# Attention and MLP decode step: each 8 MiB block as two half-transfers from two issuing engines

## The chip, the cores and the metric

The kernel runs on one core of one Trainium2 chip. Its time is device microseconds of one execution, the median of three runs. A separate execution was recorded by the hardware profiler; every number below that speaks of a line, an engine or a wait comes from that one.

## What is computed

One decode step for two sequences. A layer norm of `x` feeds two branches whose results are added to `x`: grouped-query attention over a cache of 32768 positions (32 query heads, 4 key/value heads, head size 128), and an MLP with SiLU.

```
xn  = layernorm(x)                                   # x: (2, 1, 1024)
q   = (xn @ wq) as 32 heads of 128
p   = softmax(q . k_cache * 128**-0.5)               # k_cache, v_cache: (2, 4, 32768, 128)
att = (p . v_cache) as 4096 @ wo
mlp = silu(xn @ w1) @ w2                             # w1: (1024, 3584), w2: (3584, 1024)
out = x + att + mlp
```

All of it is float32. The two caches are 268 MB, the weights some 63 MB; every byte is read once.

## The kernel before, in words

**Blocks and buffers.** The host lays out all weights and the cache as blocks of 128 rows of up to 16384 float32 (64 KiB a row, 8 MiB a block). On the chip there are two buffers of that shape, `buf[0]` (bufA) and `buf[1]` (bufB), one row per partition. Blocks alternate between them, in this order: two blocks of `wq`; `w1b` (three quarters of a block) and `w1a`; for each of the eight pairs of key/value head and sequence, two blocks of keys and two of values; two blocks of `wo`; `w2a`, in two transfers; `w2b`, in seven transfers of falling size. That makes 40 steps (`STEPS`), 20 turns of bufA and bufB.

**Loads.** SyncE issues them all (lines 110, 118 and the function `load`, L169 to L172). Each transfer of a block adds 16 to the semaphore of its buffer, `ld[0]` or `ld[1]`, when it is complete. Before it issues block n, SyncE waits until block n-2, which was in the same buffer, has been used up: `step(n)` (L166) names the semaphore and its value, `turn_sem` for the first two and `freed` for the others, which VectorE raises (`relay`, L218, through `pass_on`, L44) when TensorE has said that it is done. Two loads stand out. `x` itself (32 KiB, to every 16th partition of `xs`) is issued by ScalarE (L116), after GpSimd has cleared `xs`; and the second block is issued by SyncE only when `x` has landed (the semaphore `ldx`, L117).

**TensorE** loops over the turns. `taken(k)` (L314) waits until `ld[k]` holds 16 and takes them off again, then does the same with `tok[k]`, which says that the stationary operand `wt[k]` is ready. `slots(k, ...)` (L300) then multiplies: 64 matmuls of 128 x 32 by 128 x 512 for a full block, into the two halves of the PSUM tile `xy`. Small matmuls for the softmax follow each pair of key blocks and each pair of value blocks.

**ScalarE** works through a list in order: the issue of `x`; one square root for the layer norm (L141); for the first four blocks a copy of the PSUM result to `ev[n]` (L190 to L197); the sigmoid's exponential (L230); a copy of the queries (L239); then, for each of the eight attention rounds, a wait for `subbed` and two exponentials that make the weights for the value blocks (L245), and a wait for `normed` and a copy of the round's result, `onew` (L248); and at the end the copies of the last results (L254, L256). **VectorE** does the softmax's reductions (`attend`), **GpSimd** sets up the stationary operands (`stage`).

**The end.** The parts of `w2a` and `w2b` after the first have semaphores of their own, `more` and `last`. SyncE writes the result (L389) when ScalarE has copied it (L256).

Of the kernel before, what the change touches and what calls it, by code (L numbers as in the profile page):

```python
# [11 lines left out]
W = 16384  # L12
# [6 lines left out]
STEPS = 4 + 4 * LOOPS + 4  # L19
PAIRS = STEPS // 2  # L20
# [31 lines left out]
def gqa_plus_mlp_kernel(nc, x8, kt, v0, v1, wq, wo, w1a, w1b, w2a, w2b, out):  # L52


    pe, dve, act, pool = (Stream(nc, e, n) for e, n in
                          ((nc.tensor, "pe"), (nc.vector, "dve"), (nc.scalar, "act"), (nc.gpsimd, "pool")))
    sp, T, V, A, G = nc.sync, nc.tensor, nc.vector, nc.scalar, nc.gpsimd
    sems = [pe.sem, dve.sem, act.sem, pool.sem]

    def sem(name):  # L60
        sems.append(nc.alloc_semaphore(name))
        return sems[-1]

    def sb(name, *shape):
        return nc.alloc_sbuf_tensor(name, shape, F32).ap()
# [4 lines left out]
    buf = [sb(n, P, W) for n in ("bufA", "bufB")]  # L70
    ld, more, tok = ([sem(f"{n}{k}") for k in "AB"] for n in ("ld", "more", "tok"))
    ldx, turn_sem = (sem(n) for n in ("ldx", "marks"))
    freed, subbed, normed, tq, pself = (sem(n) for n in ("freed", "subbed", "normed", "tq", "pself"))
    trm, tgd, tls, tob = (sem(n) for n in ("trm", "tgd", "tls", "tob"))
# [39 lines left out]
    z = pool.mark(G.memset(blank, 0.0))  # L114
    act.wait(z_x)
    A.dma_start(xs[::16, :], x8).then_inc(ldx, 16)  # L116
    sp.wait_ge(ldx, 16)  # L117
    sp.dma_start(buf[1], wq[1]).then_inc(ld[1], 16)

    pool.wait(z)  # L120
    t = pool.mark(G.affine_select(out=ident, in_=ident, compare_op=ALU.not_equal, fill=1.0, base=0,
# [44 lines left out]
    def step(n):  # L166
        return (turn_sem, n) if n <= 2 else (freed, n - 2)

    def load(k, dst, src, s, n):  # L169
        if n:  # L170
            sp.wait_ge(*step(n))
        sp.dma_start(buf[k][:, dst] if isinstance(dst, slice) else dst, src).then_inc(s, 16)  # L172

    every = slice(0, W)
    load(0, slice(0, 3 * W // 4), w1b, ld[0], 1)
    load(1, every, w1a, ld[1], 2)
    for it in range(LOOPS):
        h, b = divmod(it, B)
        for j, src in enumerate((kt[b, h, 0], kt[b, h, 1], v0[b, h], v1[b, h])):
            load(j % 2, every, src, ld[j % 2], 3 + 4 * it + j)  # L180
    load(0, every, wo[0], ld[0], STEPS - 5)
    load(1, every, wo[1], ld[1], STEPS - 4)
    load(0, slice(0, W // 2), w2a[:, :W // 2], ld[0], STEPS - 3)
    load(0, slice(W // 2, W), w2a[:, W // 2:], more[0], 0)
    cuts = [0, 6 * D, 8 * D, 9 * D, 10 * D, 11 * D, 11 * D + 4 * CUT, 12 * D]
# [3 lines left out]

    for n in range(4):  # L190
        act.wait(step(n + 1))
        if n == 2:
            A.copy(ev[n][:, :512], ps[0][:, :512])
            A.copy(ev[n][:64, 512:], ps[0][:64, 512:])
            t = act.mark(A.copy(ev[n][64:96, 512:], ps[0][96:, :512]))
        else:
            t = act.mark(A.copy(ev[n], ps[n % 2]))  # L197
        if n == 1:
            pool.pass_on(tok[n], 1, t)
        else:  # L200
            pool.wait(t)
        a, b = ev[n][:, :512], ev[n][:, 512:]
        if n == 0:
            G.tensor_add(sumq[:, :512], a, b).then_inc(tok[n], 1)
        elif n == 1:
            i_sumq = pool.mark(G.tensor_add(sumq[:, 512:], a, b))  # L206
        elif n == 2:
            t = pool.mark(G.tensor_add(sumh[:96, 512:], a[:96, :384], b[:96, :384]))
            for j in range(3):
                pool.wait(t)  # L210
                t = pool.mark(G.tensor_add(sumh[96:, 512 + P * j:512 + P * (j + 1)], a[32 * j:32 * j + 32, 384:],
                                           b[32 * j:32 * j + 32, 384:]))
            shifted = t
        else:
            pool.wait(shifted)
            i_sumh = pool.mark(G.tensor_add(sumh[:, :512], a, b))
# [23 lines left out]
           tqs[:, :, ::16].rearrange("p (h m) b -> p h b m", m=REP)).then_inc(tq, 1)  # L240
    for it in range(LOOPS):
        h, b = divmod(it, B)
        act.wait((subbed, it + 1))
        for c in range(NC):
            A.activation(wt[c].rearrange("p e m -> p (e m)"), st[:, 1024 * c:1024 * c + 1024], AF.Exp,  # L245
                         scale=SCALE).then_inc(tok[c], 1)
        act.wait((normed, it + 1))
        A.copy(oT[:, REP * h:REP * (h + 1), 16 * b], onew).then_inc(tq, 1)  # L248
    for s in (trm, tgd):
# [1 line left out]
    outs = []  # L251
    for n in range(3):
        act.wait(step(STEPS - 3 + n) if n < 2 else (turn_sem, 5))
        outs.append(act.mark(A.copy(ev[n], ps[n % 2])))  # L254
    act.wait((pe, 2))
    i_ot = act.mark(A.copy(ot, acc))  # L256
# [55 lines left out]
        return m  # L312

    def taken(k):  # L314
        pe.take(ld[k], 16)
        pe.take(tok[k])

    engine = [T.engine]
# [1 line left out]
    T.reg_mov(pair, 0)  # L320
    T.reg_mov(half, 0)
    pe.wait(i_const)
    for s, n in ((trm, 1), (tgd, 1), (tls, 1), (tob, 1), (more[0], 16 * PAIRS - 16), (more[1], 16 * PAIRS - 16)):
        T.sem_inc(s, n)
    T.br("te_loop")

# [4 lines left out]
    with nc.body("te_loop", valid_engines=engine):  # L331
        again = T.mark_branch_hint_location()
        taken(0)
        slots(0, (0, 1)).then_inc(turn_sem, 1)
        taken(1)
        slots(1, (0,))
        T.br_eq(pair, PAIRS - 1, on_true="te_rest", on_false="te_more")
# [131 lines left out]
```

## Time and profile before

| | us |
|---|---|
| median of three runs | 772.4 (772.36 to 772.52) |
| the profiled execution | 772.44 |
| its span, first to last recorded work | 771.1 |
| TensorE matmuls, busy | 392.9 |
| TensorE weight loads, busy (beside the matmuls) | 125.9 |
| VectorE, busy | 133.3 |
| GpSimd, busy | 44.2 |
| ScalarE, busy | 29.0 |

The transfers moved 331.40 MB in 6816 packets, 430 GB/s over the span.

How to read the profile: PE is TensorE's matmuls, PEld its weight loads, DVE is VectorE, ACT is ScalarE, POOL is GpSimd, SP is SyncE; a name with a q (SPq, ACTq) is that engine's queue of instructions that are not counted as busy, such as the issue of a transfer. `bufA<-in_kt` means that bufA is written from the input `kt`. q1 is the queue of the transfers that SyncE issued, q10 that of those that ScalarE issued. In a row of the timeline stand the start and the duration in microseconds, then engine, line and operation, and in brackets how long the engine had been idle and what ended that. In a row of waits stand the total, the number of times and the longest. In the page's slices the span is cut into 40 equal parts.

### The profile page before, as it was taken

To read this page: it belongs to the slowest core of one execution; us is meant where nothing else is said; L and a number is where in the kernel's file an instruction comes from. 1 tells how busy PE (TensorE), PEld (TensorE's weight loads), DVE (VectorE), ACT (ScalarE), POOL (GpSimd) and SP (SyncE) were. 2 spreads that over 40 slices of the span, in tenths; PEclk is the share of its full clock that TensorE was granted. 3 is DMA by queue.
4 is the path that set the end of the run, shared out by engine and by line. 5 is a ranking of instruction groups with operands and counts; after the bars stand their busy time and mean duration, and the time that the engine had idled before them with its cause. 6 is when DMAs were issued, how large, how long until landed. Compare 5 with 4: busy or idle time off the path is not lost. (4 is left out here: it accounts for less than half of the span.)

```text
span 771.1 us, 6114 instructions
## 1 busy us (share of the span) xinstructions
PE 392.9 (51%) x2702; PEld 125.9 (16%) x2702; DVE 133.3 (17%) x100; ACT 29.0 (4%) x39; POOL 44.2 (6%) x65
## 2 busy tenths in 40 slices
PE   0454554464545454645464545454645455545476
PEld 0111111121112111211121112111211121112122
DVE  2000104030403030304030303031303030313000
ACT  0000100100010001000100010001000100010000
POOL 3001200001000000010001000100010001000121
PEclk9977667767677767677767677767677767677689
DMA  9999999999999999999999999999999999999997
GB/s 382 435 435 435 435 435 435 435 435 435 435 435 435 435 435 435 435 435 435 435 435 435 435 432 435 425 428 418 425 432 435 432 435 435 435 435 435 435 433 329
DMA packets 6816, 331.40 MB, mean 430 GB/s; under 512 B 776, under 2 KB 920, under 8 KB 1440
## 3 DMA queue, kind: packets, MB, share of 16 engines
q1 hardware_dynamic: 6800, 331.37, 99.5%
q10 hardware_dynamic: 16, 0.03, 0.0%
HBM read 331.38 MB, written 0.02 MB: 430 GB/s over the span
## 5 line engine op out<-in xcount | busy, mean ns | idle before, releaser
L107 PE MATMUL xy<-bufB,weights 128*32 128x512 f32 x1248 | 181.8, 747 | 166.6 <-PEq L49 166.6
L107 PE MATMUL xy<-bufA,weights 128*32 128x512 f32 x1280 | 178.2, 718 | 100.4 <-PEq L49 100.4
L107 PEld LDWEIGHTS xy<-bufB,weights 128*32 128x32 f32 x1248 | 49.7, 134 | 298.8 <-issue 298.7
L107 PEld LDWEIGHTS xy<-bufA,weights 128*32 128x32 f32 x1280 | 49.9, 129 | 212.1 <-issue 212.1
L268 DVE STREAM_TRANSPOSE st<-xy 128x2048 f32<-128x2048 f32 x8 | 18.5, 2317 | 241.5 <-PE xy L107 241.5
L278 DVE TENSOR_REDUCE blank<-xy 128x512 f32<-128x2048 f32 x8 | 18.3, 2292 | 224.5 <-PE xy L107 224.5
L290 POOL MEMSET weights<- 128x2048 f32 x8 | 14.4, 1805 | 526.9 <-POOLq L49 526.9
L107 PE MATMUL smA<-blank 128*8 128x128 f32 x20 | 5.4, 370 | 51.9 <-PEq L49 51.9
L107 PE MATMUL smA<-blank,ones 128*128 128x8 f32 x18 | 4.9, 347 | 50.6 <-PEq L49 50.6
L269 DVE TENSOR_REDUCE blank<-st 128x8 f32<-128x2048 f32 x8 | 30.5, 3808 | 0.3
L279 DVE TENSOR_REDUCE blank<-weights 128x8 f32<-128x2048 f32 x8 | 30.4, 3798 | 0.0
L245 ACT ACTIVATE weights<-st 128x1024 f32<-128x1024 f32 x16 | 16.0, 1048 | 326.6 <-DVE st L275 326.6
L275 DVE TENSOR_TENSOR st<-st,gmax 128x2048 f32<-128x2048 f32 x8 | 18.3, 2292 | 0.3
L107 PE MATMUL smB<-blank 128*128 128x8 f32 x72 | 15.9, 349 | 0.0
L107 PEld LDWEIGHTS smB<-blank 128*128 128x128 f32 x72 | 15.6, 317 | 0.0
L107 PEld LDWEIGHTS smA<-blank,ones 128*128 128x128 f32 x18 | 4.3, 298 | 58.5 <-issue 58.5
L248 ACT COPY blank<-onew 128x8 f32<-128x8 f32 x8 | 1.6, 204 | 279.4 <-DVE onew L282 279.4
L107 PEld LDWEIGHTS smA<-blank 128*8 128x8 f32 x20 | 1.3, 89 | 60.2 <-issue 60.2
L384 DVE TENSOR_TENSOR rest<-ev 128x512 f32<-128x512 f32 x1 | 0.7, 693 | 49.1 <-POOL ev L382 49.1
L296 POOL COPY weights<-qall 128x128 f32 x32 | 8.0, 295 | 3.1 <-POOL weights L290 3.1
L107 PE MATMUL smB<-blank,ones 8*128 8x8 f32 x20 | 5.3, 333 | 5.7 <-PEq L49 5.7
L222 DVE STREAM_TRANSPOSE tqs<-sumq 128x1024 f32<-128x1024 f32 x1 | 1.2, 1245 | 38.2 <-POOL sumq L206 38.2
(59 smaller groups left out, 59.4 us busy)
## 6 DMA issues: line engine op xcount, KB each, us to landing
bufA<-in_w2a SPq DMA_DIRECT2D x2, 4096.0 KB, 24.0
bufA<-in_w1b SPq DMA_DIRECT2D x1, 6144.0 KB, 24.8
bufB<-in_w2b SPq DMA_DIRECT2D x1, 3072.0 KB, 16.5
bufB<-in_w2b SPq DMA_DIRECT2D x3, 512.0 KB, 20.2
bufB<-in_w2b SPq DMA_DIRECT2D x1, 1024.0 KB, 18.6
bufB<-in_w2b SPq DMA_DIRECT2D x1, 384.0 KB, 21.5
bufA<-in_kt SPq DMA_DIRECT2D x8, 27.7
bufB<-in_kt SPq DMA_DIRECT2D x8, 28.9
```

What stands on the lines that cost most here:

```text
L107: return T.matmul(o, lhsT, rhs, start=start, stop=stop)
L222: i_q = dve.mark(V.transpose(tqs.rearrange("p c m -> p (c m)"), sumq))
L245: A.activation(wt[c].rearrange("p e m -> p (e m)"), st[:, 1024 * c:1024 * c + 1024], AF.Exp, scale=SCALE).then_inc(tok[c], 1)
L248: A.copy(oT[:, REP * h:REP * (h + 1), 16 * b], onew).then_inc(tq, 1)
L268: then(3, V.transpose(st, xy))
L269: V.tensor_reduce(rm, e8.rearrange("p n m -> p m n"), AX.X, ALU.max).then_inc(trm, 1)
L275: V.tensor_sub(e8, e8, gmax.to_broadcast([P, 256, REP])).then_inc(subbed, 1)
L278: V.tensor_reduce(ob, xy.rearrange("p (c n) -> p n c", c=4), AX.X, ALU.add).then_inc(tob, 1)
L279: V.tensor_reduce(lsum, weights.rearrange("p e (r m) -> p m (e r)", m=REP), AX.X, ALU.add).then_inc(tls, 1)
L290: G.memset(weights, 0.0).then_inc(pself, 1)
L296: m = G.tensor_copy(o, q[:, None, None, :].to_broadcast([P, 4, 4, REP]))
L384: t = dve.mark(V.tensor_add(rest, ev[0][:, :512], ev[0][:, 512:]))
```

## The change

Every block from the second up to the last of `wo` (numbers 1 to 37, counted from 0) is now brought by two transfers of 64 rows each into the same buffer. SyncE issues the even partitions, ScalarE the odd ones. Both add 16 to the buffer's semaphore, so TensorE now takes 32 off it. The first block, `w2a` and `w2b` remain single transfers of SyncE's; for those that `taken` waits for, the missing 16 are added by hand: by TensorE at the start for the first block, by ScalarE at the end for `w2a` and for the first part of `w2b`.

ScalarE's issues are written into its list by hand, each behind its own wait on `step`: the odd rows of the second block right after `x` (behind a wait for `ldx`, as on SyncE); those of the next four blocks ahead of the four copies to `ev[n]`; in each attention round two ahead of the wait for `subbed` and two between the exponentials and the wait for `normed`.

```diff
-    sp.wait_ge(ldx, 16)
-    sp.dma_start(buf[1], wq[1]).then_inc(ld[1], 16)
+    for eng, first in ((sp, 0), (A, 1)):
+        eng.wait_ge(ldx, 16)
+        eng.dma_start(buf[1][first::2, :], wq[1, first::2, :]).then_inc(ld[1], 16)
...
-    load(0, slice(0, 3 * W // 4), w1b, ld[0], 1)
-    load(1, every, w1a, ld[1], 2)
+    blocks = [(every, wq[0]), (every, wq[1]), (slice(0, 3 * W // 4), w1b), (every, w1a)]
     for it in range(LOOPS):
         h, b = divmod(it, B)
-        for j, src in enumerate((kt[b, h, 0], kt[b, h, 1], v0[b, h], v1[b, h])):
-            load(j % 2, every, src, ld[j % 2], 3 + 4 * it + j)
-    load(0, every, wo[0], ld[0], STEPS - 5)
-    load(1, every, wo[1], ld[1], STEPS - 4)
+        blocks += [(every, src) for src in (kt[b, h, 0], kt[b, h, 1], v0[b, h], v1[b, h])]
+    blocks += [(every, wo[0]), (every, wo[1])]
+
+    def rows(eng, n):
+        dst, src = blocks[n]
+        first = 0 if eng is sp else 1
+        eng.dma_start(buf[n % 2][first::2, dst], src[first::2, :]).then_inc(ld[n % 2], 16)
+
+    for n in range(2, STEPS - 2):
+        sp.wait_ge(*step(n - 1))
+        rows(sp, n)
...
     for n in range(4):
         act.wait(step(n + 1))
+        rows(A, n + 2)
...
     for it in range(LOOPS):
         h, b = divmod(it, B)
+        for n in (5, 6):
+            act.wait(step(4 * it + n))
+            rows(A, 4 * it + n + 1)
         act.wait((subbed, it + 1))
...
+        for n in (7, 8):
+            act.wait(step(4 * it + n))
+            rows(A, 4 * it + n + 1)
         act.wait((normed, it + 1))
...
         act.wait(step(STEPS - 3 + n) if n < 2 else (turn_sem, 5))
+        if n < 2:
+            A.sem_inc(ld[n], 16)
...
     def taken(k):
-        pe.take(ld[k], 16)
+        pe.take(ld[k], 32)
         pe.take(tok[k])
...
-    for s, n in ((trm, 1), (tgd, 1), (tls, 1), (tob, 1), (more[0], 16 * PAIRS - 16), (more[1], 16 * PAIRS - 16)):
+    for s, n in ((trm, 1), (tgd, 1), (tls, 1), (tob, 1), (ld[0], 16), (more[0], 16 * PAIRS - 16), (more[1], 16 * PAIRS - 16)):
         T.sem_inc(s, n)
```

More of the change, by code (lines that the diff above doesn't have):

```diff
@@ L171, in load @@
             sp.wait_ge(*step(n))
-        sp.dma_start(buf[k][:, dst] if isinstance(dst, slice) else dst, src).then_inc(s, 16)
+        sp.dma_start(buf[k][:, dst], src).then_inc(s, 16)
     every = slice(0, W)
-    load(0, slice(0, 3 * W // 4), w1b, ld[0], 1)
-    load(1, every, w1a, ld[1], 2)
+    blocks = [(every, wq[0]), (every, wq[1]), (slice(0, 3 * W // 4), w1b), (every, w1a)]
     for it in range(LOOPS):
         h, b = divmod(it, B)
-        for j, src in enumerate((kt[b, h, 0], kt[b, h, 1], v0[b, h], v1[b, h])):
-            load(j % 2, every, src, ld[j % 2], 3 + 4 * it + j)
-    load(0, every, wo[0], ld[0], STEPS - 5)
-    load(1, every, wo[1], ld[1], STEPS - 4)
+        blocks += [(every, src) for src in (kt[b, h, 0], kt[b, h, 1], v0[b, h], v1[b, h])]
[7 more added lines that the diff above has]
+        rows(sp, n)
     load(0, slice(0, W // 2), w2a[:, :W // 2], ld[0], STEPS - 3)
```

## The prediction

> **What bounds the kernel now.** I read the page first: which engine is busy, and what the transfers do in each of the 40 slices.
>
> ```profile
> span 771.1 us, 6114 instructions
> PE 392.9 (51%) x2702; PEld 125.9 (16%) x2702; DVE 133.3 (17%) x100; ACT 29.0 (4%) x39; POOL 44.2 (6%) x65
> GB/s 382 435 435 435 435 435 435 435 435 435 435 435 435 435 435 435 435 435 435 435 435 435 435 432 435 425 428 418 425 432 435 432 435 435 435 435 435 435 433 329
> q1 hardware_dynamic: 6800, 331.37, 99.5%
> ```
>
> No compute engine is busy for much over half of the span, while one queue's packets fill 99.5% of the sixteen transfer engines' time, at 435 GB/s in nearly every slice. The kernel is bound by moving 331.37 MB. An 8 MiB block (8.39 MB) takes 8.39 / 435 = 19.3 us.
>
> Next, the table of transfers (median time from issue to landing) and SyncE's own waits, to see how far ahead each block is asked for.
>
> ```profile
> bufA<-in_w1b SPq DMA_DIRECT2D x1, 6144.0 KB, 24.8
> bufA<-in_kt SPq DMA_DIRECT2D x8, 27.7
> bufB<-in_kt SPq DMA_DIRECT2D x8, 28.9
> bufA<-in_v SPq DMA_DIRECT2D x8, 27.1
> bufA<-in_wq SPq DMA_DIRECT2D x1, 22.2
> bufB<-in_wq SPq DMA_DIRECT2D x1, 31.4
> ```
> ```profile
> SPq L172 <- DVEq L44: 679.5, 36, 21.1
> SPq L118 <- DMA xs<-in_x: 9.7, 1, 9.7
> ```
>
> A block lands 27.1 to 28.9 us after its issue and needs 19.3 of them, so it stands queued behind its predecessor for 7.8 to 9.6 us. That is the slack: SyncE waits all the time (679.5 us) for a buffer to come free, but is told early enough that the engines never run dry. An issue may come up to 7.8 us later at no cost.
>
> **The change, part by part.** *What the sum is made against:* the profiled execution took 772.44 us, 771.1 of span and 1.3 around it; the median is 772.4. Anything within 0.2%, 1.5 us, cannot be told from no change.
>
> *ScalarE's new waits and issues.* 37 blocks are split (wq's second, w1b, w1a, 32 cache blocks, two of wo): 36 of 8.39 MB and one of 6.29, 308.3 MB together, 308.3 / 435 = 709 us of the run; half, 154.1 MB, moves to ScalarE's queue. One cache round and the head show what ScalarE has to do around the points of issue.
>
> ```profile
> 0.74 0.38 SPq L110 DMA_DIRECT2D bufA<-in_wq  x1
> 1.71 1.13 ACTq L116 DMA_DIRECT2D xs<-in_x  x1
> 2.88 1.28 ACT L141 ACT_TABLE_LOAD   x1 [2.88 <-issue]
> 10.83 0.33 SPq L118 DMA_DIRECT2D bufB<-in_wq  x1
> 12.59 0.20 ACT L141 ACTIVATE ln<-ln 128x1 f32<-128x1 f32 x1 [8.43 <-DVE ln L139]
> 16.04 0.21 DVE L161 COPY weights<-xT 128x128 f32<-128x128 f32 x1
> 23.19 7.07 PE L107 MATMUL xy<-bufA,weights 128*32 128x512 f32 x48 [23.19 <-PEq L49]
> ...
> 32.03 0.33 SPq L172 DMA_DIRECT2D bufA<-in_w1b  x1
> ```
> ```profile
> 356.31 0.33 SPq L172 DMA_DIRECT2D bufB<-in_v  x1
> 367.10 2.00 ACT L245 ACTIVATE weights<-st 128x1024 f32<-128x1024 f32 x2 [39.76 <-DVE st L275]
> 377.02 0.33 SPq L172 DMA_DIRECT2D bufA<-in_kt  x1
> 396.13 0.33 SPq L172 DMA_DIRECT2D bufB<-in_kt  x1
> 405.10 0.20 ACT L248 COPY blank<-onew 128x8 f32<-128x8 f32 x1 [35.99 <-DVE onew L282]
> ```
>
> An issue costs SyncE 0.33 us and cost ScalarE 1.13 us once; I take 0.33 to 1.13 each. Queued behind a round's second issue (356.3) stand the exps, whose input comes at 367.1; behind its fourth (396.1) stands the copy of onew, due at 405.1. The cover is 8.97 us or more against at most 1.13, and the order of ScalarE's waits is that in which the buffers come free, so no issue waits behind work of a later one. Were the cover gone, 1.13 us of each issue would still lie inside the 7.8 of slack. Cost: nothing. TensorE now waits for 32 counts, the later of the two halves; its matmuls are all that queues behind, and that is the same slack.
>
> *Completion packets.* 37 more transfers bring 37 x 16 = 592 small packets. The slices that now hold a block's end still show 435, so an end costs under 0.5 GB/s of a 19.3 us slice, 0.02 us; 37 of them under 0.8 us, more likely 0.3.
>
> *The head.* ScalarE now waits for xs ahead of its square root. At worst its table load, too, moves behind that wait: 10.83 + 1.13 + 1.28 = 13.24 instead of 12.59, so the first weights are ready at 16.9 instead of 16.25, and the first matmul needs them at 23.19. Nothing. But the odd rows of the second block no longer queue behind the first block: they are on a queue of their own and take turns with it, as xs did (issued at 1.71, landed by 10.83, long before the block issued at 0.74). They are 4.19 MB, 9.6 us. The first block then lands up to 9.6 us later and w1b is issued at up to 41.7 instead of 32.03; the second block still lands at 10.83 + 31.4 = 42.2. The transfer that has nothing ahead of it, the first, took 22.2 us, 2.9 over 19.3. So a bubble of 0 to 41.7 + 2.9 - 42.2 = 2.4 us; rows already under way when the odd half arrives go ahead of it, so I take 0.
>
> *The tail* is issued by SyncE alone as before. ScalarE's two additions to the counts stand ahead of copies that it makes anyway, some 20 us before TensorE needs them. Nothing.
>
> *Sharing the sixteen engines.* This term decides. Per block, each engine carries eight rows of 64 KB; afterwards four from each queue, in turns. The trace of before holds one place with a second queue: the rows of xs. I asked the transfer view for windows that each catch the start of sixteen rows, one an engine: 4.7 to 5.4 us (ahead of xs), 7.2 to 7.9 (beside its rows), 9.6 to 10.4 (beside its completions). The last column is packet time as a share of sixteen engines in the window.
>
> ```profile
> q1 hardware_dynamic: 16, 1.05, 345.6%
> ```
> ```profile
> q1 hardware_dynamic: 16, 1.05, 352.6%
> q10 hardware_dynamic: 8, 0.03, 11.4%
> ```
> ```profile
> q1 hardware_dynamic: 16, 1.05, 302.7%
> q10 hardware_dynamic: 8, 0.00, 0.6%
> ```
>
> A row alone takes 3.456 x 0.70 = 2.419 us, and 3.027 x 0.80 = 2.422 when a completion of the other queue goes in between: taking turns costs at most 3 ns, over 37 x 8 = 296 rows 0.9 us. Beside the eight rows of xs, 0.114 x 0.70 x 16 = 1.28 us of packets in all, it takes 3.526 x 0.70 = 2.468 us: 49 ns more for each of sixteen, 0.78 us. So a microsecond of such packets costs the others 0.61 us, though blocks' own rows run sixteen abreast without slowing one another. What is different about xs is where its rows go: eight rows, one an engine, to every 16th partition, so into parts of the memory where another engine is writing.
>
> Will the halves' rows do that? A full block's sixteen engines clearly keep to parts of their own. xs shows rows handed out by their number in the transfer, one each, and not by partition. Handed out so, the 64 even rows give each engine four that are spread over eight partitions; the rows that one engine has today may well be chosen to lie in its own part, and four rows of every second partition then reach into the part of another. The trace holds no 64-row transfer, so the bounds are wide: 0 if every engine still has its part to itself; with two engines always in one part, and nothing gained by it, each row takes twice its time, 709 us more. In between lies the measured price: 0.61 x 709 = 433 us. I take that one, the only row for such sharing. The sum: 772.4 + 433 + 0.3 = 1205 us, rounded, with 772.4 + 709 = 1481 as its upper end; a lower end of 800 allows for engines that drift apart and then meet seldom.
>
> The Trainium skill, SBUF — State Buffer, section "Door 1: The DMA port swizzle", names such parts: sixteen ports, each of two groups of four neighbouring partitions. DMA: Bandwidth & Descriptors, "The descriptor swizzle", gives each engine one port in a 128-partition transfer. If the 64 rows are dealt four in a row, two engines meet on a port while another port idles: by that the block takes twice 19.3 us, 1481 us in all. The trace agrees as far as xs goes; no run here shows the dealing of 64 rows.
>
> **The rivals.**
> *No difference.* The dealing of a half gives each engine rows in a part that no other writes (or the parts carry more than one engine's stream), and the halves simply take turns. For it: the turns cost nothing, the slack covers every issue, and eight partitions an engine are as many as now. Against it: the 0.61. It decides if rows in the middle stay under 2.43 us. 772.4 + 0.3 = 772.7 us, from 771 to 773.9. This is also what comes out if the queues do not mix and one half goes after the other.
> The Trainium skill, DMA: Bandwidth & Descriptors, "Issuing engines are not separate DMA queues", has it so: the issuers' transfers interleave on the same sixteen engines, and only issue time is saved. By that it is 772.4 us.
>
> *A little slower.* The rows do not collide, but the head's bubble (2.4), the ends (0.8) and the turns (0.9) come at their full price: 772.4 + 4.1 = 776.5 us. For it: the odd half does get in front of the first block. Against: the bubble needs all four odd rows of an engine to pass.
>
> *Faster.* A second queue closes the gap between rows. 2.419 us a row is 16 x 65,536 / 2.419 us = 433.5 GB/s, and no slice shows over 435: at most 0.35% of 709, 2.5 us, 770 us. Against it: rows with the other queue's packets between them took no less than 2.419.
>
> **How the numbers follow.** Collisions, 1205 us: 0.47, on the price of xs and on dealing by number. No difference: 0.36. A little slower: 0.11. Faster: 0.06. Slower is 0.47 + 0.11 = 0.58. The forecast's own range is 800 to 1481; as the next case holds 0.36, the range for 8 in 10 must reach it: 771 to 1481, which leaves out the faster case and little else.
>
> **What would show it.** Right: middle slices near 435 / 1.61 = 270 GB/s with the engines still busy, rows near 3.9 us, a block each 31 us instead of 19.3, SyncE and ScalarE issuing within a microsecond of one another. q10 holding 37 x 64 rows and 154 MB shows only that the change does what it says. Wrong: 435 in the slices and rows of 2.42 us (no difference), or rows of 4.8 us (each part wholly shared, 1481). A gap in the DMA line near 42 us would be the head's bubble. An issue of ScalarE's more than 7.8 us behind SyncE's would mean that its order of work, and not the memory, costs the time.

## The result and the profile after

| | before | after |
|---|---|---|
| median of the runs, us | 772.46 (6 runs) | 775.64 (6 runs, 774.99 to 776.87) |
| ratio to before | | 1.0042, 95% interval 1.003 to 1.0055 |
| profiled execution, us | 772.44 | 775.31 |
| its span, us | 771.1 | 774.0 |

The kernel became 3.2 us slower. The forecast had been 1205 us; the rival "a little slower", at 776.5 us, came nearest. From the page of the kernel after:

```profile
span 774.0 us, 6154 instructions
GB/s 381 434 379 434 434 434 434 434 434 434 434 434 434 434 434 434 434 434 434 434 434 434 434 434 434 434 434 434 434 434 434 434 434 434 434 434 434 434 430 329
q1 hardware_dynamic: 4432, 177.23, 53.2%
q10 hardware_dynamic: 2976, 154.18, 46.0%
```

The change does what it says: 154 MB went over ScalarE's queue. And one slice out of forty is different: the third reads 379. Stages of equal length side by side, first of the kernel after, then of the kernel before (the last two columns are the share of the sixteen transfer engines and GB/s):

```profile
38.70:58.05 19.35, 10.64 (x100) 3.55 (x92) 1.25 (x1) 2.02 (x2) 2.54 (x2) 0.89 0.92 379
58.05:730.00 671.95, 345.55 (x2362) 111.20 (x2362) 125.77 (x84) 22.07 (x31) 28.09 (x47) 0.73 1.00 434
```
```profile
38.70:58.05 19.35, 10.83 (x76) 3.50 (x80) 1.25 (x1) 1.01 (x1) 1.26 (x1) 0.76 1.00 434
58.05:730.00 671.95, 346.99 (x2358) 111.63 (x2350) 125.76 (x84) 23.08 (x32) 29.14 (x48) 0.73 1.00 434
```

In the 672 us of the cache both move 434 GB/s, so no row became longer there, nor did a turn between the queues cost anything. The trace also keeps the start and the duration of every row (its packet records), and they say the same: a row of 64 KB takes 2.42 us in both, the kernel after is 2.7 us behind when 20 MB have been moved and still 2.6 us behind at 330 MB. In the stage from 38.7 us, (434 - 379) / 434 x 19.35 = 2.45 us are lost, of the 2.9 us by which the span grew. What happened there is in the timeline of the kernel after (start, duration, engine, line, operation):

```profile
10.65 0.56 SPq L119 DMA_DIRECT2D bufB<-in_wq  x1
10.66 0.51 ACTq L119 DMA_DIRECT2D bufB<-in_wq  x1
32.95 8.84 PE L107 MATMUL xy<-bufA,weights 128*32 128x512 f32 x64 [32.95 <-PEq L49]
41.84 0.47 SPq L185 DMA_DIRECT2D bufA<-in_w1b  x1
42.64 7.07 PE L107 MATMUL xy<-bufB,weights 128*32 128x512 f32 x64 [0.86 <-PEq L49]
```

The first block used to be multiplied from 23.19 us on, and now from 32.95. So its buffer comes free, and w1b is issued, at 41.84 instead of 32.03 us, just as the second block has landed (its matmuls start at 42.64). The view of the transfers in a window from 40 to 46 us shows the hole, in slices of 0.15 us that count packets by their start; the second fence is a window from 43.0 to 44.2:

```profile
DMA  0000000000000000000099900989000000070979
```
```profile
q1 hardware_dynamic: 16, 0.79, 219.8%
```

No row starts between 40 us and 43.1, which is 1.3 us after the issue, and the sixteen rows that then start (48 KB each, 0.79 MB) take 2.198 x 1.2 = 2.64 us each, instead of 2.42 x 48 / 64 = 1.82. By the packet records the second block's last rows end between 41.24 and 41.90 and these rows start between 43.10 and 44.12, so that an engine stands idle for 1.8 us on average. Hole and slow restart together are 1.8 + 0.8 = 2.6 us; the 2.45 is what a view gives that counts rows by their start.

The table of transfers (median time from issue to landing) shows why the first block was late:

```profile
bufA<-in_kt SPq DMA_DIRECT2D x8, 24.3
bufA<-in_kt ACTq DMA_DIRECT2D x8, 27.5
bufA<-in_wq SPq DMA_DIRECT2D x1, 31.9
bufB<-in_wq SPq DMA_DIRECT2D x1, 22.2
bufB<-in_wq ACTq DMA_DIRECT2D x1, 31.7
```

The first block takes 31.9 us instead of 22.2, 9.7 more, which is the time of half a block. (Where two transfers add to one semaphore, this table books the first 16 counts to the one issued first. The rows SPq and ACTq of bufB therefore say only that one half was there at 10.65 + 22.2 = 32.9 us and the other at 42.4; the queues below show that ScalarE's was the earlier one.) All four odd rows of each engine went ahead of the first block's completion: three ahead of its last row, the fourth ahead of its completion packets, which wait for a turn like any row. The transfer views of three windows, 26.4 to 27.6, 28.8 to 30.0 and 31.3 to 32.4 us, show the end of it (packets that start there, MB, and their time as a share of the engines' window):

```profile
q1 hardware_dynamic: 16, 1.05, 201.8%
```
```profile
q10 hardware_dynamic: 16, 1.05, 201.9%
```
```profile
q1 hardware_dynamic: 32, 1.05, 221.0%
q10 hardware_dynamic: 16, 0.00, 0.8%
```

First come the sixteen last rows of the first block, SyncE's, one an engine; then ScalarE's fourth odd row of each engine; and then the completion packets of both queues (16 each, nearly no bytes) with SyncE's next sixteen rows. In the steady part the halves of a key block need 24.3 and 27.5 us, so the later one lands as a whole block did before.

### The profile page after: what moved, and what is told of

It reads as the page before. It is cut to its first block, busy times and chain, and to the rows that moved or that the text cites. A ratio compares the mean times of both kernels' runs of the same rounds, so it can differ in the third digit from the quotient of the medians.

```text
span 774.0 us, 6154 instructions
## 1 busy us (share of the span) xinstructions
PE 388.3 (50%) x2702; PEld 124.7 (16%) x2702; DVE 133.3 (17%) x100; ACT 29.0 (4%) x39; POOL 44.2 (6%) x65
## 2 busy tenths in 40 slices
DMA packets 7409, 331.41 MB, mean 428 GB/s; under 512 B 1368, under 2 KB 1512, under 8 KB 2032
## 5 line engine op out<-in xcount | busy, mean ns | idle before, releaser
L107 PE MATMUL xy<-bufB,weights 128*32 128x512 f32 x1248 | 176.1, 727 | 158.0 <-PEq L49 158.0
## 6 DMA issues: line engine op xcount, KB each, us to landing
bufA<-in_kt SPq DMA_DIRECT2D x8, 24.3
```

Of the source, the lines that this page charges most:

```text
L107: return T.matmul(o, lhsT, rhs, start=start, stop=stop)
```

## The experiments

Thirteen kernels beside the change, against the kernel before on the same chip.

**1. The second block whole again.** The first theory was that the gap belongs to the second block's odd half ("head"), against a cost at every split block ("everywhere").

```diff
-    for eng, first in ((sp, 0), (A, 1)):
-        eng.wait_ge(ldx, 16)
-        eng.dma_start(buf[1][first::2, :], wq[1, first::2, :]).then_inc(ld[1], 16)
+    sp.wait_ge(ldx, 16)
+    sp.dma_start(buf[1], wq[1]).then_inc(ld[1], 16)
```

> The second block comes whole from SyncE again; all later blocks stay split. Theory 'head': the loss is the gap after the second block, because its odd rows pass the first block; with them gone the first matmul starts near 23.2 us again, the third slice of the page reads 434 instead of 379, and the time is 772.4 plus at most 0.5 for the added completions: 772.5 to 773.0 us. Rival 'everywhere': two queues cost something at each of 37 split blocks; 36 of them are left, so the time stays near 775.5 us.

Measured: 775.94 us, ratio 1.0041 (1.0027 to 1.0054). By the number the rival wins; by the profile neither is right. The timeline:

```profile
22.98 9.74 PE L107 MATMUL xy<-bufA,weights 128*32 128x512 f32 x64 [22.98 <-PEq L49]
32.78 0.56 SPq L184 DMA_DIRECT2D bufA<-in_w1b  x1
47.80 9.28 PE L107 MATMUL xy<-bufB,weights 128*32 128x512 f32 x64 [15.08 <-PEq L49]
57.14 0.47 SPq L184 DMA_DIRECT2D bufB<-in_w1a  x1
57.52 7.07 PE L107 MATMUL xy<-bufA,weights 128*32 128x512 f32 x64
```

The first block is on time. But now the first odd half is that of w1b, it passes the rest of the second block, and that one is used from 47.80 instead of about 42.5; w1a is issued at 57.14, when w1b is all but there. The gap has moved one block on: the slice from 38.7 us reads 359. So the theory was widened to "empty queue": where ScalarE's queue is empty while SyncE's still holds rows, the next odd half passes them.

**2. Only the second block split.**

```diff
     def rows(eng, n):
-        first = 0 if eng is sp else 1
-        eng.dma_start(buf[n % 2][first::2, dst], src[first::2, :]).then_inc(ld[n % 2], 16)
+        if eng is sp:
+            eng.dma_start(buf[n % 2][:, dst], src).then_inc(ld[n % 2], 16)
+        else:
+            eng.sem_inc(ld[n % 2], 16)
```

> The other half of the change: only the second block is split, all later ones come whole from SyncE (ScalarE adds their missing counts at the places where it issued). Theory 'head': the gap is there as before, first matmul near 32.9 us, third slice near 379, 774.8 to 775.4 us. Rival 'everywhere': one split block of 37 costs under 0.1 us, 772.4 to 772.6 us.

Measured: 775.04 us, 1.0036 (1.0022 to 1.005). The first matmul starts at 32.84 and the stage reads 393:

```profile
38.70:58.05 19.35, 10.69 (x100) 3.60 (x92) 1.25 (x1) 2.02 (x2) 2.53 (x2) 0.89 0.94 393
```

The stage was expected near 379, but the time is as expected: one split block of 37 makes 2.6 of the 3.2 us. With experiment 1: the first split costs, whichever it is, and the parts do not add up, since each alone has its own first split.

**3. Both halves from SyncE.**

```diff
...
-        first = 0 if eng is sp else 1
-        eng.dma_start(buf[n % 2][first::2, dst], src[first::2, :]).then_inc(ld[n % 2], 16)
+        for first in range(2 if eng is sp else 0):
+            eng.dma_start(buf[n % 2][first::2, dst], src[first::2, :]).then_inc(ld[n % 2], 16)
```

> Even and odd halves of all 37 blocks as in the change, but both issued by SyncE, one behind the other on one queue. Theory 'head': the odd rows of the second block stand behind the first block, so no gap: 772.5 to 773.0 us, the same number of transfers and completions as in the change. Rival 'dealing': 64-row transfers of every second partition are themselves slower, on whatever queue: 775 us or more.

The second block is changed in the same way. Measured: 772.82 us, 1.0006 (0.9997 to 1.0015), first matmul at 23.16. The same 64-row transfers, on one queue, cannot be told from the kernel before. It is the second queue that costs, not the halves.

**4. A larger dose.** ScalarE issues the whole second block right behind xs.

```diff
-    for eng, first in ((sp, 0), (A, 1)):
-        eng.wait_ge(ldx, 16)
-        eng.dma_start(buf[1][first::2, :], wq[1, first::2, :]).then_inc(ld[1], 16)
+    A.dma_start(buf[1], wq[1]).then_inc(ld[1], 16)
...
```

> A larger dose: ScalarE issues the whole second block, all eight rows of each engine, right behind xs and without waiting for it; later blocks stay split. Theory 'head': its rows take turns with the first block from about the third row on, so some six instead of four of them go ahead of the first block's last row. The first matmul starts at about 36 to 38 us instead of 32.9, w1b is issued 3 to 5 us later than the 41.84 of the change, and the second block still ends near 41.5: the gap grows to 5 to 8 us and the time to 778 to 781 us. Rival 'everywhere': 775.5 us, as in the change.

Measured: 783.21 us, 1.0145 (1.013 to 1.0161), 2.2 us more than the most that was expected. The first block is used from 39.85 us and w1b issued at 49.02:

```profile
39.85 9.11 PE L107 MATMUL xy<-bufA,weights 128*32 128x512 f32 x64 [39.85 <-PEq L49]
49.02 0.56 SPq L183 DMA_DIRECT2D bufA<-in_w1b  x1
```

Seven rows' time later than before (39.85 - 23.19 = 16.7 us, 16.7 / 2.42 = 6.9) instead of four. A larger dose of passing moves the loss from 3.2 to 10.8 us.

**5. Why the collisions did not come: other halves.** SyncE brings partitions 0 to 63, ScalarE 64 to 127; then the same with both on SyncE's queue.

```diff
...
-        eng.dma_start(buf[n % 2][first::2, dst], src[first::2, :]).then_inc(ld[n % 2], 16)
+        eng.dma_start(buf[n % 2][64 * first:64 * first + 64, dst], src[64 * first:64 * first + 64, :]).then_inc(ld[n % 2], 16)
```

> The change with other halves: SyncE brings partitions 0 to 63 of a block, ScalarE 64 to 127. This asks why the collisions that were forecast did not come. Theory 'ports': parts of the memory take one engine's stream at a time, and the dealing of even rows happens to keep engines apart; rows of one half of the partitions cannot, since sixteen engines then share the parts of eight: rows of up to 4.8 us, 1100 to 1500 us. Rival 'room': a part of the memory carries two engines' streams, so which rows an engine gets does not matter: rows of 2.42 us and 775 to 776 us, as in the change.

> The same halves, partitions 0 to 63 and then 64 to 127, both issued by SyncE on one queue, so that all sixteen engines surely work on one half at a time. Theory 'ports': twice the time for each block, near 1480 us, at most 10% less where engines get out of step. Rival 'room': 772.5 to 773 us.

Measured: 1512.51 us, 1.9532 (1.9451 to 1.9614), on two queues, and 1550.82 us, 2.0074 (2.0041 to 2.0108), on one, both a little above what was expected. The stage from 60 to 1450 us of each:

```profile
60.00:1450.00 1390.00, 351.42 (x2374) 112.97 (x2378) 127.00 (x85) 23.07 (x32) 29.27 (x48) 0.61 1.00 211
```
```profile
60.00:1450.00 1390.00, 350.32 (x2364) 112.06 (x2364) 126.62 (x83) 22.86 (x31) 27.25 (x46) 0.61 1.00 207
```

The engines are busy all the time (share 1.00) and move 211 and 207 GB/s instead of 434. Two queues help little, as the engines stay in step: in the packet records of the first kernel, all sixteen rows under way belong to one and the same queue at 732 of 800 points of time between 200 and 600 us. So 64 rows that crowd into half of the partitions cost twice the time. This fits parts of the memory that take one stream at a time; the rows read changed along with the rows written, and these two runs alone do not separate the two. The Trainium skill has such parts in SBUF — State Buffer, section "Door 1: The DMA port swizzle" (some 218 GB/s for partitions 0 to 63); the trace agrees. The Trainium skill, DMA: Bandwidth & Descriptors, "Rules for kernel authors", says of two transfers to disjoint partition halves that they serialize, and advises against them; here they cost 1.95 to 2.0 times one whole transfer when the halves are top and bottom, and nothing that can be measured (experiment 3) when they are even and odd on one queue.

**6. The price of crossing rows by itself.** The kernel before, with 32 extra transfers of 8 rows of 8 KB from ScalarE into a spare tile that nothing uses, four in each round; in the second kernel the partitions are 0, 16, 32 to 112.

```diff
+    def side(m):
+        for n in (m, m + 1):
+            act.wait(step(n + 5))
+            if n:
+                A.wait_ge(at_side, 16 * n)
+            A.dma_start(spare[0:32:4, :], wo[0, :8, :2048]).then_inc(at_side, 16)
...
+        side(4 * it)
...
+        side(4 * it + 2)
...
```

> The kernel before, with 32 extra transfers of 8 rows of 8 KB issued by ScalarE (four in each attention round) into a spare tile, partitions 0, 4, 8 to 28; the result does not use them. It is the control for the run with partitions 0, 16, 32 to 112. Each adds 8 rows of some 0.30 us, one each on eight of the engines, which makes these eight the slower ones by 32 x 0.30 = 9.7 us. Both theories: 772.4 + 9.7 = 782 us.

> The same 32 extra transfers into partitions 0, 16, 32 to 112, as xs has them: rows that go where other engines are writing. It measures the price of 0.61 us per us by itself. Theory 'ports': the engines that own those parts lose what two of the rows take, 0.60 us each time, 32 x 0.60 = 19 us instead of 9.7: 785 to 792 us, and the blocks' rows next to them are longer by 0.1 us or more. Rival 'room': the same as the control within 0.5 us, and the 49 ns seen beside xs came from something else at that place.

Measured: 783.16 us, 1.0139 (1.0122 to 1.0156), and 802.61 us, 1.0395 (1.0378 to 1.0413); from 130 to 690 us the first moves 432 GB/s and the second 420. The control adds 10.8 us, 0.34 for each transfer; one such row takes 0.31. Crossing adds another 802.61 - 783.16 = 19.45 us, 0.61 a transfer, more than the expected 785 to 792 us allows. The source is the same in both, so where the rows are written makes the difference. The blocks' rows next to one side transfer show how; the first fence is the crossing kernel from 188.6 to 189.4 us, the second the control from 188.8 to 189.4. Each catches the start of eight rows that are under way when the side rows start, at 189.88 to 190.21 and at 190.16 to 190.42:

```profile
q1 hardware_dynamic: 8, 0.52, 188.2%
```
```profile
q1 hardware_dynamic: 8, 0.52, 202.2%
```

The share is that of sixteen engines, and eight rows start, so a row takes 1.882 x 0.80 x 2 = 3.01 us, against 2.022 x 0.60 x 2 = 2.43 in the control. By the packet records the other eight engines' next rows, from 190.19 to 190.75, take 2.76 to 3.00 us. So every one of the sixteen engines loses 0.3 to 0.6 us beside eight crossing rows, and not only the owners of the parts that these enter, as the theory "ports" of the expectation had it. What makes the others wait no run shows. The same holds for the place from which the prediction took its 0.61: beside xs all sixteen rows are longer, 2.448 to 2.564 us instead of 2.42.

**7. Quarters on one queue.** Each block in four transfers of every fourth partition, from SyncE.

```diff
...
-        first = 0 if eng is sp else 1
-        eng.dma_start(buf[n % 2][first::2, dst], src[first::2, :]).then_inc(ld[n % 2], 16)
+        for first in range(4 if eng is sp else 0):
+            eng.dma_start(buf[n % 2][first::4, dst], src[first::4, :]).then_inc(ld[n % 2], 16)
...
-        pe.take(ld[k], 32)
+        pe.take(ld[k], 64)
...
```

> Each of the 37 blocks in four transfers of every fourth partition (32 rows, two an engine), all from SyncE on one queue. It asks two things. Completions: halves on one queue cost 0.4 us for 37 more transfers, so 111 more should cost 1.1 to 1.2: 773.4 to 773.8 us. Dealing: if a strided transfer's rows are dealt so that every engine keeps to its own part whatever the stride, rows stay at 2.42 us; if even rows were a lucky case, engines meet and the time goes to 1000 us or more.

Measured: 772.87 us, 1.0007 (0.9998 to 1.0016). The expectation of 1.1 us for the completions missed: 111 more transfers cost no more than 37 (772.82), and neither can be told from nothing. On the dealing it was clear: 32 rows of every fourth partition collide no more than 64 of every second. Rows of a strided transfer that reaches over all partitions do not get in one another's way; by which rule they are dealt to the engines no run shows.

**8. The first block split too.** If both queues hold rows from the start, nothing should pass.

```diff
-    sp.dma_start(buf[0], wq[0]).then_inc(ld[0], 16)
+    sp.dma_start(buf[0][0::2, :], wq[0, 0::2, :]).then_inc(ld[0], 16)
...
+    A.dma_start(buf[0][1::2, :], wq[0, 1::2, :]).then_inc(ld[0], 16)
...
```

> The first block is split too (ScalarE issues its odd rows right behind xs), the rest as in the change. After the run with a whole second block, in which the gap only moved one block on, theory 'head' is widened to theory 'empty queue': wherever ScalarE's queue is empty while SyncE's still holds rows, the next odd half passes them, the block ahead lands late, its buffer comes free late and the engines run dry. With the first block split both queues hold rows from the start: no gap, third slice 434, 772.6 to 773.1 us (0.4 for the completions, as with both halves on one queue). The first matmul may start late, near 28 us, as xs now stands behind fewer rows of its own queue or more; the slack covers that. Rival 'two queues': two queues in turn leave a gap at the start whatever the order: 775 us or more.

Measured: 774.85 us, 1.003 (1.0018 to 1.0041): a miss. The first matmul starts at 30.67, w1b is issued at 39.85:

```profile
GB/s 381 434 430 434 434 434 427 434 430 434 434 434 434 434 434 434 434 434 434 434 434 434 434 434 434 434 434 434 434 434 434 434 430 434 434 434 434 415 424 318
30.67 9.12 PE L107 MATMUL xy<-bufA,weights 128*32 128x512 f32 x64 [30.67 <-PEq L49]
39.85 0.48 SPq L186 DMA_DIRECT2D bufA<-in_w1b  x1
```

ScalarE's half was issued at 2.91, behind xs, when SyncE's, issued at 0.74, was under way. So now SyncE's queue was ahead, and the second block's even rows passed the first block's odd ones, by 30.67 - 23.19 = 7.5 us, three rows. That is close to the slack, and the third slice lost little (430). The last three slices, though, read 415, 424 and 318 instead of 434, 430 and 329 in the change. The packet records sort the 2.5 us that this execution's stream ends behind the kernel before: 0.3 us by the first rows, 0.7 at w1b (engines idle 0.3 us on average, first rows 0.4 longer), some 0.4 between 95 and 235 us, and 1.1 in the last 1.2 MB, where the change loses 0.4. So a small gap at w1b came even here; what costs the 0.4 and the 1.1 was not found.

**9. The odd half issued when the first block has landed.** Nothing is left to be passed at the second block.

```diff
+    sp.dma_start(buf[0][0::2, :], wq[0, 0::2, :]).then_inc(ld[0], 16)
+    sp.dma_start(buf[0][1::2, :], wq[0, 1::2, :]).then_inc(landed, 16)
...
+    sp.dma_start(buf[1][0::2, :], wq[1, 0::2, :]).then_inc(ld[1], 16)
...
     t = act.mark(A.activation(std, var, AF.Sqrt))
+    A.wait_ge(landed, 16)
+    A.dma_start(buf[1][1::2, :], wq[1, 1::2, :]).then_inc(ld[1], 16)
...
```

> All 37 blocks split between SyncE and ScalarE as in the change; the one difference is that ScalarE issues the odd rows of the second block when the first block has landed (SyncE brings that one in two halves, the later with a semaphore of its own) and not when xs has. Theory 'empty queue': nothing is left of the first block to be passed, and both queues hold rows when w1b is issued: first matmul near 23.2 us, third slice 434, 772.5 to 773.1 us. Rival 'two queues': 774.8 us or more, as in the run with the first block split too.

Measured: 774.96 us, 1.0032 (1.002 to 1.0044): a miss again, and again the timeline shows a passing, a block later:

```profile
25.01 8.62 PE L108 MATMUL xy<-bufA,weights 128*32 128x512 f32 x64 [25.01 <-PEq L49]
33.68 0.47 SPq L188 DMA_DIRECT2D bufA<-in_w1b  x1
46.26 9.93 PE L108 MATMUL xy<-bufB,weights 128*32 128x512 f32 x64 [12.64 <-PEq L49]
56.25 0.47 SPq L188 DMA_DIRECT2D bufB<-in_w1a  x1
```

ScalarE's odd rows, issued at 23.57 us, started some rows behind the even ones, so SyncE's queue ran empty first and the even rows of w1b, issued at 33.68, passed them. The second block was used at 46.26 and w1a issued at 56.25; the slice from 58.0 us reads 383. In the packet records the engines stand idle for 1.4 us on average there, and the first rows after that take 3.1 us instead of 2.42: 2.1 of the 2.6 us.

**10. Splitting only from block 20, and only from block 21 on.**

```diff
...
-        first = 0 if eng is sp else 1
-        eng.dma_start(buf[n % 2][first::2, dst], src[first::2, :]).then_inc(ld[n % 2], 16)
+        if n >= 20:
+            first = 0 if eng is sp else 1
+            eng.dma_start(buf[n % 2][first::2, dst], src[first::2, :]).then_inc(ld[n % 2], 16)
+        elif eng is sp:
+            eng.dma_start(buf[n % 2][:, dst], src).then_inc(ld[n % 2], 16)
+        else:
+            eng.sem_inc(ld[n % 2], 16)
```

> Blocks up to the 19th whole from SyncE, blocks 20 to 37 split. Theory 'empty queue': the odd half of block 20 passes the last three or four rows of block 19 on each engine; block 19 lands 7 to 10 us late, the buffer for block 21 comes free that much later, and a gap of 1 to 3 us appears once, near 440 us, and none near 42: 773.5 to 776 us. Rival 'start only': the gap belongs to the first blocks, where rows are slow and the LayerNorm waits: 772.5 to 772.8 us.

> Blocks up to the 20th whole, 21 to 37 split: one block later than in the run from the 20th on. Again odd rows pass the block ahead, here block 20, the first keys of a round; its matmuls wait for their weights until 408.4 us in the kernel before, some 3 us after it has landed, and the block after it ends near 424.4. Two or three rows of delay make its buffer free at 419 to 422 instead of 417.5, still ahead of that by more than the 1.2 us from issue to first row. Theory 'empty queue, less the slack': no gap, 772.4 to 773.0 us. Rival 'each start of splitting costs': as from the 20th on, 773.5 to 774.5 us.

Measured: 774.03 us (772.68 to 774.9), 1.002 (1.001 to 1.0031), and 772.90 us, 1.0008 (0.9999 to 1.0017). Of the first the profiled execution was one of its shortest, 772.81 us: block 19 is used at 390.91 instead of 386.06, the next issue comes at 400.07 instead of 396.13, still inside the slack, and the page's line of the transfer engines stays at nine tenths or more up to the last slice. So the passing is shown there and the gap is not. Of the second kernel the profiled execution was the longest of eleven, 773.97 us (another took 773.91, the rest 772.59 to 773.38):

```profile
412.65 10.01 PE L107 MATMUL xy<-bufA,weights 128*32 128x512 f32 x64 [8.34 <-PEq L49]
424.75 8.77 PE L107 MATMUL xy<-bufB,weights 128*32 128x512 f32 x64 [2.08 <-PEq L49]
```

Block 20 is used 4.3 us late (408.39 before), its successor at 424.75 as before (424.76). But block 20's buffer comes free late too: SyncE issues the next block into it at 422.78 instead of 417.54, and block 21's last rows end at 423.66 to 423.98, 0.9 to 1.2 us after that. The views from 421.6 to 424.0 us and from 424.0 to 424.6 show what follows:

```profile
q1 hardware_dynamic: 16, 0.00, 0.4%
```
```profile
q1 hardware_dynamic: 16, 1.05, 522.8%
```

First there are completion packets only, and then sixteen rows of 5.228 x 0.60 = 3.14 us instead of 2.42. With the 0.4 us for which an engine stands idle on average, that is 1.1 us, by which this execution exceeds the median. So the gap of the head came here too, in the middle of the cache, at a delay that just used up the slack. That the slower executions of the kernel from block 20 have it as well is inferred. With the median at 772.90, 17 blocks on two queues in turn otherwise cost nothing that can be measured. No kernel tried is faster than the one before.

## Why the prediction was wrong, point by point

**What bounds the kernel, and the slack: right.** The engines are full, and the later half of a cache block lands in 27.3 to 29.3 us against 27.1 to 28.9.

**ScalarE's issues: right.** They cost 0.50 us each, within the 0.33 to 1.13; the exps follow 10.8 us behind the second issue of a round as before, and no issue came late.

**Completions and turns: right.** 0.3 and at most 0.9 us had been allowed; experiments 3, 7 and 10 show under 0.6 by their medians, and the packet records of the change show no growth from 20 to 330 MB. (The page's slices could not have shown 0.02 us: they count rows by their start, and eight rows an engine fall into a slice.)

**The head: the mechanism and the bound were right, the value taken was not.** The step that failed is "rows already under way when the odd half arrives go ahead of it, so I take 0". All four odd rows passed: the first block 9.7 us late (9.6 at most, it had said), w1b issued at 41.84 (41.7), a loss of 2.45 us in the slice and 2.7 in the packet records (2.4). Rows under way do not lessen this: behind those under way the first block still had enough rows to come for three odd rows to go in between, and the fourth went ahead of its completion. Experiments 1, 2 and 4 move this loss and scale it.

**Sharing the sixteen engines: wrong, and it carried the forecast.** The step that failed is "four rows of every second partition then reach into the part of another", and with it the 0.61 x 709 = 433 us. In its place the rows of the halves took 2.42 us, as whole blocks' rows do, and the term is zero. Such a price can be real: with top and bottom halves the time went to 1512 and 1551 us, somewhat above the 1481 that was set as the end. But rows of every second or fourth partition over the full height do not collide, as experiments 3 and 7 show. xs had shown that rows crossing into other parts cost something; it had not shown that a half would cross. Nor did the cost fall on the owners of those parts alone: all sixteen rows beside xs were longer (experiment 6), so what stands behind the 0.61 is open. That a half would cross was an assumption about a transfer that the trace did not contain, and it was given 0.47.

**The chances.** "A little slower" got 0.11 for being built from worst cases. One of its three terms was all but settled by arithmetic that stood in the text: four rows in strict turns, 9.6 us, against the 7.3 us that the same paragraph left (42.2 - 2.9 - 32.03). That its 776.5 lies within a microsecond of the 775.6 is in part luck: the other two terms, 1.7 us, did not come, and the bubble cost a little more than its 2.4.

## What to carry to other kernels

Two queues into the same ring of buffers are not one queue twice as wide: they take turns row by row, so whichever holds less lets its next transfer pass what is still waiting in the other. The block that is passed lands late, its buffer comes free late, and beyond the slack the transfers run dry, once, at the place where the queues become uneven; so ask at each start of a split what stands in the other queue, and compare its delay with the slack. Split a block over its partitions only in a way that lets each transfer reach over the full height: even and odd cost nothing, top and bottom twice the time.

## What the runs showed of the hardware

- Partitions 0 to 63 and 64 to 127 as transfers of their own: 207 to 211 GB/s, on one queue or two, with all sixteen engines busy. Every second or every fourth partition: 434 to 435 GB/s.
- A transfer of eight rows of 8 KB to partitions 0, 16, ... 112 costs 0.95 us of the kernel's time ((802.61 - 772.36) / 32), the same rows to partitions 0, 4, ... 28 cost 0.34. Beside the former, rows of all sixteen engines took 2.76 to 3.06 us instead of 2.42.
- After a gap, the first row starts 1.3 us after the issue (41.84 to 43.10, and 422.78 to 424.03), and the first rows are slow: 2.64 us instead of 1.82 for 48 KB, 3.14 instead of 2.42 for 64 KB.
- A completion packet takes its turn behind a row of the other queue: the first block's last rows started at about 26.9 us and its completion came with the packets at about 31.7, one 64 KB row of ScalarE's (2.4 us) between them.
- 111 more transfers, with 16 completions each, made no difference that can be measured (772.87 against 772.82 us).
